# RWKV-6 and an MLP mixer on one core: the guarding branch at the end of the kernel, turned around, and a prefetch hint on TensorE

## The chip, the cores and the metric

The kernel runs on one core of one Trainium2 chip. The metric is the time of one launch on the device, in microseconds, as the median of several runs. A core has five engines with an instruction stream each: TensorE (PE; its weight loads are listed as PEld), VectorE (DVE), ScalarE (ACT), GpSimd (POOL) and SyncE (SP), which here issues nearly all transfers. [...] A profile is one further execution, recorded by the hardware. "q8" and "q14" in it are the queues on which the engines' own instructions are brought in.

## What is computed

Four sequences of 768 tokens pass through a linear attention with decay and then through a mixer over tokens and channels:

```python
for t in range(S):                      # B, H, S, D = 4, 8, 768, 48
    cur = einsum('bhd,bhe->bhde', u[None] * k[:, :, t], v[:, :, t])
    y[:, :, t] = einsum('bhd,bhde->bhe', r[:, :, t], state + cur)
    state = w[:, :, t][:, :, :, None] * state + einsum('bhd,bhe->bhde', k[:, :, t], v[:, :, t])
x = y.transpose(0, 2, 1, 3).reshape(B, S, H * D)                # 4 x 768 x 384
h = maximum(x.transpose(0, 2, 1) @ w_tok1, 0) @ w_tok2          # 768 -> 256 -> 768, over tokens
u = x + h.transpose(0, 2, 1)
out = u + maximum(u @ w_ch1, 0) @ w_ch2                         # 384 -> 1536 -> 384, over channels
```

## The kernel before

The attention is worked off in twelve units (four sequences, three units of 256 tokens each), and the mixer of a sequence follows its units. The fast way through the attention takes products of decays over a chunk of 64 tokens and divides by them. That is sound only while these products stay within a range. So each unit leaves two sums in `flags` (`ranges`, L343), which are zero when all its products lay in the range, and the kernel ends with a guard: when any flag is set, everything is computed again in another way that holds for any decay (`by_halves`, L773, in a loop over the four sequences, L838 to L840). I call this the general path. With the inputs at hand no flag is set and the general path is never entered.

The order of issue of the straight part is written out by hand: `strict` (L88) runs a list of small functions and ties every instruction to the one ahead of it on its engine. The lists are made of pieces, pairs of a weight and a function; `woven` mixes several lists in proportion to the weights. The last sequence's mixer has a list of its own, `last_mixing` (L726). Its tail is:

- `quarters(0)`, the second product of the channel mixer for rows 0 to 255, and after it `verdict` (L714): one matmul adds up the flags, VectorE reduces the 24 sums to one (L719) and turns it into a whole number, 0 or 1 (L720);
- the first product of the channel mixer for the last third of the rows;
- `quarters(1)` and `quarters(2)`, rows 256 to 511 and 512 to 767.

`quarters(s)` computes two 128-row blocks with seven products in place of eight. A product is a run of matmuls into one of two PSUM buffers (`q_ps`, L607), 24 instructions on TensorE as the trace lists them (12 weight loads, 12 matmuls), which a VectorE addition or a ScalarE copy takes out. The list it gives back has 11 pieces, in this order:

```python
return [(1.96, p1), (0.01, lambda: dve.tensor_add(s1, a21, a22)), (1.96, p4),
        (0.01, lambda: dve.tensor_sub(s2, s1, a11)), (1.96, p2), (0.01, lambda: dve.tensor_sub(a21, a11, a21)),
        (1.96, p5), (0.01, lambda: dve.tensor_sub(s4, a12, s2)), (1.96, p6), (1.96, p7), (1.96, p3)]
```

`p7` stores one row block and `p3`, the last, the other (L611, on SyncE's queue). The additions that take out the products are L617 (p1), L621 (p4), L625 (p2), L629 (p5), L633 and L634 (p6), L639 and L640 (p7) and L645 (p3).

After the straight part each engine loads the verdict into a register of its own (`values_load`, L768) and comes to the guard (L838). In the profile the guard's instructions stand on that line: compare-and-branch instructions, and waits on semaphores[...]. The program's own end follows the guard in the code; its last waits, its drains and the barrier over all engines have the line of the closing of the context, L871.

Of the kernel before, what the change touches and what calls it, by code (L numbers as in the profile page):

```python
# [12 lines left out]
i32 = mybir.dt.int32  # L13
# [3 lines left out]
ALU = mybir.AluOpType  # L17
# [28 lines left out]
def woven(*lists):  # L46

    keyed = []
    for n, pieces in enumerate(lists):
        total, at = sum(c for c, _ in pieces), 0.0  # L50
        for i, (c, f) in enumerate(pieces):
            keyed.append(((at + c / 2) / total, n, i, c, f))
            at += c
    return [(c, f) for *_, c, f in sorted(keyed, key=lambda e: e[:3])]
# [8 lines left out]
def rwkv6_then_mixer(  # L63
# [17 lines left out]
    nc = tc.nc  # L81
    pe, dve, act, pool, sp = nc.tensor, nc.vector, nc.scalar, nc.gpsimd, nc.sync
# [16 lines left out]
    const = ctx.enter_context(tc.tile_pool(name="const", bufs=1))  # L99
# [564 lines left out]
    def mixing_of(bt):  # L664
        return mixing(bt, lambda: xs[bt], lambda n: out[bt, ts(n, 128), :])
# [46 lines left out]
    flagged = []  # L712

    def verdict():  # L714
        total = bank("total")[0:1, :2 * NU]
        pe.matmul(total, ones, flags.rearrange("p i n -> p (i n)"), start=True, stop=True)
        of_all = const.tile([128, 1], f32, name="of_all")
        beyond = const.tile([128, 1], i32, name="beyond")
        dve.tensor_reduce(out=of_all[0:1], in_=total, axis=mybir.AxisListType.X, op=ALU.add)  # L719
        dve.tensor_scalar(beyond[0:1], of_all[0:1], 0.0, 1.0, op0=ALU.is_le, op1=ALU.is_lt)  # L720
        flagged.append(beyond)

    def bank(name):
        return ps_c.tile([128, 512], f32, name=name, tag="c")

    def last_mixing():  # L726
        hiddens, turned, rights, thirds, quarters = mixing_of(B - 1)
        of, sums = rights(0)
        *turned, end = turned
        pieces = [e for h in hiddens for e in h] + turned[:8] + sums[:4] + turned[8:10] + sums[4:8] + turned[10:] + sums[8:]  # L730
        ups = thirds(0, of)
        of, sums = rights(1)
        pieces += ups[:2] + [end] + ups[2:4] + woven(ups[4:], sums) + thirds(1, of)

        def third():
            L["of"], L["sums"] = rights(2)

        L = {}
        sums = [(0.05, lambda n=n: L["sums"][n][1]()) for n in range(12)]
        lefts_of = [(0.9, lambda n=n: L["ups"][n][1]()) for n in range(15)]  # L740
        pieces += [(0.01, third)] + woven(quarters(0), sums) + [(0.1, verdict), (0.01, lambda: L.update(ups=thirds(2, L["of"])))]
        return pieces + lefts_of + quarters(1) + quarters(2)

    for bt in range(B):
        ahead = []
        if bt == 0:
            to_ch = [single(e, n) for n, e in enumerate(to_ch)]
            both = [f for e in zip(ups[0], ups[1]) for f in e]
            ahead = woven(turned, sum(to_ch[:2], []))
            of_weights = [(0.1, lambda n=n: weight_sums(n)) for n in range(4)]  # L750
            pieces = woven(both, sum(to_ch[2:8], [])) + woven(downs[0][:6], to_ch[8]) + woven(downs[0][6:], of_weights[:3])
            pieces += downs[1][:4] + of_weights[3:] + downs[1][4:] + ups[2] + downs[2]
        elif bt < B - 1:
            hiddens, turned, ups, downs = mixing_of(bt)
            pieces = [e for h in hiddens for e in h] + turned
            *pieces, last = pieces
            ups[0].insert(2, last)
            for s in range(S // SEG):
                pieces += ups[s] + downs[s]
        else:  # L760
            six_banks.close()
            ps_c = six_banks.enter_context(tc.tile_pool(name="ps_c", bufs=6, space=bass.MemoryType.PSUM))
            pieces = last_mixing()
        n = (bt + 1) * UB
        att = [e for i in range(n, n + UB) if i < NU for e in steps(i)]
        strict(*(f for _, f in ahead + (woven(att, pieces) if att else pieces)))

    rare = nc.values_load(flagged[0][0:1, 0:1], min_val=0, max_val=1, skip_runtime_bounds_check_because="a comparison's result")  # L768

    six_banks.close()  # L770
    ps_g, ps_a = for_attention()
# [63 lines left out]
        for s in range(S // SEG):  # L835
            emit(ups[s] + downs[s])

    with tc.If(rare > 0, preferred_fallthrough_block=False):  # L838
        with tc.For_i(0, B, 1) as b:
            by_halves(b)  # L840

# [33 lines left out]
```

## Time and profile before

| What | us |
|---|---|
| Median of three runs | 548.63 |
| Lowest and highest of them | 548.43, 549.2 |
| The profiled execution, its own time | 550.15 |
| Its span, first to last instruction | 548.4 |
| TensorE busy in the span | 507.8 |

The profiled execution took 1.5 us more than the median of the runs; times inside it add up to its own total, not to the median. TensorE's granted clock is 0.977 of full speed over the span, and full from 122 us on. "Busy" leaves out branches, register loads, waits on semaphores and the issue of transfers. These belong to an engine's sequencer and are listed with a small q behind the engine's name; several parts of the end of this kernel consist of nothing else.

The registers of the verdict are loaded at L768 at quite different times, since each engine comes there when its own stream is through: GpSimd at 502.2 us, ScalarE at 530.7, TensorE at 539.3, VectorE at 542.4 and SyncE at 543.1.

### The profile page before, as it was taken

The page shows a single profiled execution, that of the slowest core. Times are in us where ns is not written, and L with a number is a line of the kernel's source. Part 1 is how long each engine was busy: PE and PEld are TensorE (multiplying, and loading weights), DVE is VectorE, ACT ScalarE, POOL GpSimd, SP SyncE. Part 2 cuts the span into 40 slices and gives each one's busy share as a digit, 9 for nine tenths or more (in the row PEclk, how much of TensorE's full clock was granted, in tenths as well). Part 3 has the DMA queues.
Part 4 walks back from the last instruction along what each step waited for, and adds up shares of the span by engine and source line. Part 5 has one row for each costly group of instructions (what it writes and reads, how often), then busy time and mean ns, then how long its engine had stood idle before and what let it go on. Part 6 is the DMA issues. An engine that isn't in the chain of part 4 may idle for free.

```text
span 548.4 us, 12596 instructions
## 1 busy us (share of the span) xinstructions
PE 507.8 (93%) x5542; PEld 435.3 (79%) x5542; DVE 335.8 (61%) x504; ACT 212.7 (39%) x525; POOL 1.3 (0%) x10
## 2 busy tenths in 40 slices
PE   3569899899799999999899999999999999999995
PEld 3556578666698868888888967888888968999995
DVE  7997599878772754192380665295393525775653
ACT  3676776662233333423323324413414313431300
POOL 0000000000000000000000000000000000000000
PEclk9678999899999999999999999999999999999999
DMA  8956656622231403203123113002000000000000
GB/s 304 330 165 209 182 178 241 172 89 84 87 108 34 139 17 117 59 32 125 46 78 92 45 44 99 30 1 88 1 30 1 2 29 2 1 1 31 0 31 33
DMA packets 20941, 46.01 MB, mean 84 GB/s; under 512 B 2128, under 2 KB 13008, under 8 KB 20880
## 3 DMA queue, kind: packets, MB, share of 16 engines
q1 hardware_dynamic: 20736, 45.14, 25.4%
q8 instruction: 45, 0.74, 0.6%
q14 instruction: 16, 0.13, 0.1%
q10 hardware_dynamic: 144, 0.00, 0.0%
HBM read 40.41 MB, written 4.72 MB: 82 GB/s over the span
## 4 chain that ended last, share of the span: by engine, by line
PE 72%; DVE 17%; ACT 6%; DMA 3%; issue 2%; SPq 0%; DVEq 0%; ACTq 0%
PE q_ps L607 21%; PE z_ps L518 21%; PE z_ps L550 6%; PE h_ps L494 5%; PE h_ps L501 4%; PE h_ps L589 3%; PE y_ps L306 3%; DVE to_end L354 3%; PE y_ps L320 2%; PE gram L248 2%; DMA rk<-in_rk_dram 2%; PE kv_ps L293 2%; PE gram L276 1%; DVE z L649 1%; ACT before L416 1%
## 5 line engine op out<-in xcount | busy, mean ns | idle before, releaser
L518 PE MATMUL z_ps<-xT,wch 128*128 128x256 f32 x648 | 149.1, 385 | 1.1 <-DVE o L645 1.1
L518 PEld LDWEIGHTS z_ps<-xT,wch 128*128 128x128 f32 x648 | 120.8, 191 | 18.9 <-DVE o L645 1.9
L607 PE MATMUL q_ps<-wch,z 128*128 128x192 f32 x492 | 87.4, 329 | 0.7 <-DVE o L629 0.5
L607 PEld LDWEIGHTS q_ps<-wch,z 128*128 128x128 f32 x492 | 80.3, 190 | 2.6 <-DVE o L629 1.1
L520 ACT ACTIVATE z<-z_ps 128x256 f32<-128x256 f32 x108 | 41.3, 382 | 84.8 <-PE z_ps L518 84.2
L607 PE MATMUL q_ps<-scratch,z 128*128 128x192 f32 x324 | 57.1, 328 | 3.5 <-DVE o L625 2.9
L607 PEld LDWEIGHTS q_ps<-scratch,z 128*128 128x128 f32 x324 | 52.9, 190 | 4.8 <-DVE o L625 3.8
L416 ACT ACTIVATE before<-state,to_end 112x48 f32<-112x48 f32 x176 | 44.2, 324 | 30.6 <-DVE state L426 28.0
L426 DVE TENSOR_TENSOR state<-before,kv_ps 112x192 f32<-112x192 f32 x40 | 14.0, 350 | 45.1 <-ACT before L416 29.0
L494 PE MATMUL h_ps<-x,wtok 128*128 128x384 f32 x96 | 33.9, 506 | 2.4 <-ACT x L326 2.0
L501 PE MATMUL h_ps<-h,wtok 128*128 128x384 f32 x96 | 35.4, 493 | 0.1
L503 DVE TENSOR_TENSOR x<-x,h_ps 128x384 f32<-128x384 f32 x24 | 13.3, 553 | 33.6 <-PE h_ps L501 33.4
L617 DVE TENSOR_TENSOR o<-x,z 128x192 f32<-128x192 f32 x8 | 2.9, 358 | 49.8 <-ACT z L616 46.7
L494 PEld LDWEIGHTS h_ps<-x,wtok 128*128 128x128 f32 x96 | 18.3, 195 | 14.6 <-ACT x L326 2.8
L354 DVE TENSOR_TENSOR_SCAN to_end<-w,starts 112x1041 f32<-112x1041 f32 (+1 forms) x13 | 28.1, 2160 | 2.0 <-DMA w<-in_w_dram 1.6
L362 DVE TENSOR_TENSOR_SCAN w<-w,starts 112x1041 f32<-112x1041 f32 x12 | 27.9, 2321 | 0.1
L346 ACT ACTIVATE junk<-to_end,least 112x1041 uint8<-112x1041 f32 x12 | 13.9, 1162 | 28.3 <-DVE to_end L354 28.3
L501 PEld LDWEIGHTS h_ps<-h,wtok 128*128 128x128 f32 x96 | 16.6, 190 | 9.6 <-ACT h L496 2.5
L326 ACT COPY x<-y_ps 64x384 f32<-64x384 f32 (+1 forms) x36 | 17.1, 475 | 18.3 <-PE y_ps L320 18.0
L306 PEld LDWEIGHTS y_ps<-before,rk 48*64 48x64 f32 x704 | 14.0, 144 | 12.3 <-issue 10.2
L306 PE MATMUL y_ps<-before,rk 48*64 48x48 f32 x704 | 15.4, 230 | 8.0 <-DVE state L426 8.0
L511 ACT COPY xT<-xT_ps 128x384 f32<-128x384 f32 x24 | 11.4, 476 | 22.0 <-PE xT_ps L510 22.0
(139 smaller groups left out, 668.3 us busy)
## 6 DMA issues: line engine op xcount, KB each, us to landing
rk<-in_rk_dram SPq DMA_DIRECT2D x36, 192.0 KB, 3.7
near<-in_near_dram SPq DMA_DIRECT2D x8, 768.0 KB, 4.5
w<-in_w_dram SPq DMA_DIRECT2D x11, 520.5 KB, 3.4
spare<-in_w_ch_dram SPq DMA_DIRECT2D x10, 512.0 KB, 4.8
vt<-in_v_dram SPq DMA_DIRECT2D x12, 384.0 KB, 3.8
out_dram<-o SPq DMA_DIRECT2D x24, 192.0 KB, 1.9
scratch<-in_w_ch_dram SPq DMA_DIRECT2D x8, 512.0 KB, 4.4
rk<-in_rk_dram SPq DMA_DIRECT2D x6, 512.0 KB, 8.4
```

Of the source, the lines that this page charges most:

```text
L306: pe.matmul(y[put(q, j), q, ds((c * A + a) * D, D)], r_[q * P:q * P + D, ds((c * A + a) * 128 + j * T, T)], before[g][q * P:q * P + D, a, ...
L326: return [lambda: act.copy(x[:, 0], got[:, 0])] + [lambda n=n: act.copy(x[ts(n, P), 1], got[ts(1 - n, P), 1]) for n in range(2)]
L354: dve.tensor_tensor_scan(to, of, start, 0.0, op0=ALU.mult, op1=ALU.add)
L362: dve.tensor_tensor_scan(w_[:ROWS], w_[:ROWS], starts[:ROWS], 0.0, op0=ALU.mult, op1=ALU.add)
L416: act.mul(t[:ROWS, a], state[bt, g][:ROWS, a], by_last(c, j)[:, a:a + 1])
L494: pe.matmul(sums[i], wtok1[:, c, ts(i, 128)], x_of()[:, c, :], start=(c == 0), stop=(c == C - 1))
L501: pe.matmul(ps, wtok2[:, i, ts(c, 128)], h1[:, i, :], start=(i == 0), stop=(i == DTOK // 128 - 1))
L518: pe.matmul(ps, wch1[:, m, ts(jt, 128)], xT[:, m, ts(s, SEG)], start=(m == 0), stop=(m == DM // 128 - 1))
L520: act.activation(zs[s][:, jt, :], ps, AF.Relu)
L550: pe.matmul(ps[:, q], lefts[r][:, ts(q, 128)], of[r], start=first and q == 0, stop=end and q == JB - 1, skip_group_check=True)
L589: pe.matmul(ps, zs[0][:, jt, ts(n, 128)], wch2[:, jt, :], start=(jt == 0), stop=(jt == NJ - 1))
L607: pe.matmul(ps, a[:, j, :], b[:, j, :], start=(j == 0), stop=(j == HJ - 1))
```

## The change

The verdict's number is turned around: it was 1 when a flag was set and is now 1 when none is. The guard asks for that and has an empty branch for it; the general path becomes the `Else`. In both versions the block for "false" is asked for as the one that follows the branch in the code. Before, "false" meant the end of the kernel; now it means the general path, and the block for "true", for which the general path has to be jumped over, lies behind it.

A branch hint, "LikelyTaken", for the guard's branch, which gets the label `by_halves`, is put in TensorE's stream only. It stands in the list of `quarters(2)` five pieces ahead of the end, and so just ahead of `p5`. `quarters(2)` is now called ahead of `quarters(1)`, but the pieces run in the order they had.

```diff
-        beyond = const.tile([128, 1], i32, name="beyond")
+        within_range = const.tile([128, 1], i32, name="within_range")
         dve.tensor_reduce(out=of_all[0:1], in_=total, axis=mybir.AxisListType.X, op=ALU.add)
-        dve.tensor_scalar(beyond[0:1], of_all[0:1], 0.0, 1.0, op0=ALU.is_le, op1=ALU.is_lt)
-        flagged.append(beyond)
+        dve.tensor_scalar(within_range[0:1], of_all[0:1], 0.0, None, op0=ALU.is_le)
+        flagged.append(within_range)
...
-        return pieces + lefts_of + quarters(1) + quarters(2)
+        ending = quarters(2)
+        ending.insert(-5, (0.01, lambda: tc.mark_branch_hint_location("by_halves", "LikelyTaken", [pe.engine])))
+        return pieces + lefts_of + quarters(1) + ending
...
-    rare = nc.values_load(flagged[0][0:1, 0:1], min_val=0, max_val=1, skip_runtime_bounds_check_because="a comparison's result")
+    common = nc.values_load(flagged[0][0:1, 0:1], min_val=0, max_val=1, skip_runtime_bounds_check_because="a comparison's result")
...
-    with tc.If(rare > 0, preferred_fallthrough_block=False):
+    with tc.If(common > 0, preferred_fallthrough_block=False, label="by_halves") as within_range:
+        pass
+    with within_range.Else():
         with tc.For_i(0, B, 1) as b:
             by_halves(b)
```

## The prediction, made before the changed kernel was run

> **What bounds the kernel now.** I read the page first, then the chain of waits from 535 us on, then the guard's own line (L838) and the program's closing line (L871) on every engine, then the last stores, and last the DMA records of the final microseconds.
>
> The page says that TensorE sets the time nearly everywhere, and that two queues carry nothing but instructions, q8 in pieces of 16 KB and q14 in pieces of 8 KB:
>
> ```profile
> span 548.4 us, 12596 instructions
> ...
> PE 507.8 (93%) x5542; PEld 435.3 (79%) x5542; DVE 335.8 (61%) x504; ACT 212.7 (39%) x525; POOL 1.3 (0%) x10
> ...
> q8 instruction: 45, 0.74, 0.6%
> q14 instruction: 16, 0.13, 0.1%
> ```
>
> The chain ends with the last matmul's consumer, the VectorE addition at L645, at 542.37 + 0.35 = 542.72 us:
>
> ```profile
> 534.86 7.49 PE q_ps L607 x46
> 542.35 0.02 issue
> 542.37 0.35 DVE o L645
> ```
>
> The span ends at 548.44. So 5.7 us follow in which nothing computes, and only there can a turned branch act. The guard's line and the closing line, by engine (a count, then min/median/max in ns, then first and last start in us):
>
> ```profile
> L838 ACTq COMPARE_BRANCH  x2: 38/42/45, 531.3 to 531.7; - x2
> L838 PEldq COMPARE_BRANCH  x2: 95/1954/3813, 539.9 to 542.5; - x2
> L838 DVEq COMPARE_BRANCH  x2: 51/53/55, 543.0 to 543.2; - x2
> L838 SPq COMPARE_BRANCH  x2: 38/44/49, 543.7 to 546.6; - x2
> ```
>
> ```profile
> L871 ACTq DRAIN  x2: 8/44/81, 534.2 to 548.0; - x2
> ...
> L871 SPq EVENT_SEMAPHORE  x10: 17/28/28, 547.1 to 548.4; - x10
> ```
>
> Every engine runs two branches: one that is not taken, then its waits on semaphores, then one that is taken over the general path. TensorE's second takes 3813 ns; after SyncE's second, at 546.64, its next instruction comes at 547.12. Now the stores of the last two row blocks (this view covers 500 us on):
>
> ```profile
> L611 SPq DMA_DIRECT2D out_dram<-o x6: 332/332/333, 500.4 to 542.8; - x6
> ...
> DMA to landing us min/median/max: 1.9/1.9/3.6
> ```
>
> Five land in about 1.9 us; the longest, 3.6, is the last, issued at 542.75 and landed at 546.36. SyncE's eight waits at L838 show who minds: four stand at 543.80 to 544.04, the fifth, on this store's semaphore, ends at 546.37. What the transfer does meanwhile stands in the windows (last two columns: DMA share of 16 engines, GB/s):
>
> ```profile
> 543.50:544.30 0.80, 0.00 (x0) 0.00 (x0) 0.00 (x0) 0.00 (x0) 0.00 (x0) 1.00 0.61 230
> 544.30:544.95 0.65, 0.00 (x0) 0.00 (x0) 0.00 (x0) 0.00 (x0) 0.00 (x0) 1.00 0.07 15
> 544.95:545.85 0.90, 0.00 (x0) 0.00 (x0) 0.00 (x0) 0.00 (x0) 0.00 (x0) 1.00 0.06 12
> ```
>
> A share of 0.06 is one engine of sixteen. The trace's packet records name it: a 16 KB packet of q8 runs from 543.478 to 544.923; 15 of the store's 16 parts have finished by 544.264; eight 1536-byte packets follow one after another from 544.918 and end at 545.884. TensorE's branch, which starts at 542.524, fetches its target, and the fetch stands ahead of a sixteenth of the last store. Thus two things end together: TensorE's stall (its drain starts at 546.395) and the store.
>
> [...] TensorE needs 3.87 us from the branch to its drain, ScalarE 2.52 (531.72 to 534.24); VectorE, SyncE and GpSimd[...] need 0.57, 0.48 and 0.45. [...] the held part starts as the fetch ends. [...]
>
> **The change part by part.**
>
> *The verdict.* The same VectorE instruction with one operation instead of two; 142 ns at 502.0 us, 40 us ahead of its last reader's use. Nothing.
>
> *The hint.* One instruction in TensorE's stream ahead of product p5 of the last block. TensorE's sequencer runs ahead: p3's buffer is free at 538.82 and its 24 instructions are issued by 539.27. So p2, whose buffer is free at 531.03, is issued by about 531.5, and the hint follows while 2 us of p2 and more before it are queued: hidden, cost 0. From there to the branch at 539.86 are 8.4 us against 3.87 for a fetch. No trace of before shows a hint; bounds: below, nothing; above, one whole stall of 3.87 without cover. I take 0. Its fetch at about 532.5 meets no store: those of the block before landed by 530.95, the next begin at 542.2.
>
> *The far branch, on TensorE.* It becomes the first one, 539.86, which the sequencer reaches while 2.5 us of matmuls are queued. Hinted, it should take some 0.5 us. Even if the hint did nothing, the fetch would lie at 540.81 to 542.26 (0.95 after the branch, 1.45 long) and the branch end at 543.7: away from the last store, whose packets start at 543.59, and early enough for the closing barrier. So the stall goes off the end either way.
>
> *The last store.* With no fetch ahead of it all sixteen parts should be done by 544.26; the fifteen others report by 544.62. SyncE's wait ends at about 544.63 instead of 546.37: −1.74. What is late next? SyncE itself: its register load is done at 543.64, its branch at 543.70 is now taken (0.48 instead of 0.10), its waits start at 544.18 and it comes to the fifth at 544.49. Just in time, 0.14 us ahead of the landing.
>
> *SyncE's second branch.* Today 0.48 us stand between 546.64 and 547.12, on the path that ends. If the common target runs on into the end of the program, this goes: −0.48. If a jump remains: 0. I take −0.48, since a branch over a block is what makes a second one necessary now, and the new target lies behind that block.
>
> *The other engines.* VectorE's taken branch moves from 543.20 to 543.00[...]. Bounds 0 and +0.54; I take 0. ScalarE's stall of 2.5 us at 531 and GpSimd's branch at 503 have over 10 us of cover in either order.
>
> Sum: −1.74 − 0.48 = −2.22. The closing waits and the barrier (547.12 to 548.44) stay as they are. The profiled execution took 550.15: 548.44 of span and 1.71 around it. It would take 546.22 + 1.71 = 547.93. The median shown is 548.63, 1.52 below the profiled one; the same saving gives 546.4.
>
> **The rivals.**
>
> *A, as worked out*: 546.4, own range 545.8 to 547.1 (the three runs before span 0.8). Chance 0.70.
>
> *B, a part only*: VectorE's fetch takes the place of TensorE's in front of the last packets (+0.54), a jump remains (+0.48), or both: −1.7 to −1.2, down to −0.5 if some other piece of the closing turns up late: 547.0 to 548.1. For it: the margin of SyncE is 0.14 us, and VectorE's fetch comes 0.1 us ahead of the store's end. Against: one DMA engine in sixteen. Chance 0.14.
>
> *C, no gain to be seen*: [...] At ScalarE's price (2.52) its waits start at 546.22, the fifth passes at once, and the closing waits start at about 546.8 instead of 547.12: −0.3, so 548.3. For it: the change moves the target by some ten instructions. Against: the distance over the general path is the same, and SyncE's jump made it without a stall today. The same time results if the collision is an affair of the profiled execution alone. Chance 0.08.
>
> *D, slower*: [...] Before, no fetch lies between 522.30 and 543.48, [...] with nothing queued to cover it all of this stands on the path: −2.22 + 3.87 = +1.65, 550.3. It decides from a loss of 2.2 + 1.1 = 3.3 us up. Against: two microseconds of queued product usually cover part of it. Chance 0.08.
>
> **How the numbers follow.** A has 0.70, B 0.14, C 0.08, D 0.08. The likeliest is A, 546.4. With A, and B nearly whole, less their tails, the range 545.8 to 548.1 holds about 0.8. A measurement here tells 0.2%, 1.1 us, from no change: faster means below 547.5. A nearly whole and two thirds of B: 0.79. Within 0.2%: the rest of B, C and a bit of D: 0.13. Slower: D, 0.08.
>
> **What would show it.** Right: one branch per engine at L838 where there were two; none of TensorE's above 1 us; a 16 KB packet on q8 near 532; the last store landing in about 1.9 us; SyncE's closing waits starting near 544.9. Hint without effect but A still true: TensorE's branch at 539.9 takes 3.8 us and the end is early all the same. B: a second branch on SyncE, or a lone 8 KB packet ahead of the store's last ones. C: SyncE's branch followed by a gap of 2.5 us. D: a gap in TensorE's products between 531 and 540. Wrong altogether: the last store still lands after 546.

## The result, and the profile after

The changed kernel takes 547.14 us (median of eight runs, 545.73 to 547.86), the kernel before 548.58 in the same comparison (eight runs, 548.06 to 549.2). The ratio is 0.9968, with a 95% interval of 0.9953 to 0.9983: faster by 1.4 us, by this measurement somewhere between 0.9 and 2.6. The profiled execution took 547.47 us with a span of 545.8.

The guard's line, L840 now, on four engines of the changed kernel (a count, then min/median/max in ns, then first and last start in us), with the hint, which the trace puts on the closing's line:

```profile
L840 ACTq COMPARE_BRANCH  x1: 50/50/50, 530.8 to 530.8; - x1
L840 ACTq EVENT_SEMAPHORE  x1: 17/17/17, 533.4 to 533.4; - x1
L840 PEldq COMPARE_BRANCH  x1: 397/397/397, 539.4 to 539.4; - x1
...
L840 DVEq COMPARE_BRANCH  x1: 72/72/72, 542.6 to 542.6; - x1
...
L840 SPq COMPARE_BRANCH  x1: 45/45/45, 543.3 to 543.3; - x1
```

```profile
L875 SPq EVENT_SEMAPHORE  x10: 17/28/28, 544.5 to 545.7; - x10
...
L875 PEldq BRANCH_PREFETCH_HINT  x1: 45/45/45, 531.0 to 531.0; - x1
```

Where each engine ran two branches there is one. TensorE's takes 397 ns where its second one took 3813. SyncE's closing waits begin at 544.5, right behind its last wait at the guard:

```profile
L840 SPq EVENT_SEMAPHORE  x8: 17/17/17, 543.8 to 544.4; - x8
```

The stores from 500 us on:

```profile
L611 SPq DMA_DIRECT2D out_dram<-o x6: 332/332/333, 499.9 to 542.3; - x6
...
DMA to landing us min/median/max: 1.8/1.9/2.0
```

The longest is no longer 3.6 us. The windows of the last store (last three columns: granted clock, DMA share of 16 engines, GB/s) show all its parts together:

```profile
543.10:543.85 0.75, 0.00 (x0) 0.00 (x0) 0.00 (x0) 0.00 (x0) 0.00 (x0) 1.00 0.71 262
543.85:544.75 0.90, 0.00 (x0) 0.00 (x0) 0.00 (x0) 0.00 (x0) 0.00 (x0) 0.59 0.05 18
```

What is left in the second window are two pieces of 8 KB on q14 (543.95 to 544.26 and 544.34 to 544.75); the store's last packet ends at 543.84. The chain of waits still closes with the same addition:

```profile
541.93 0.02 issue
541.95 0.35 DVE o L645
```

From its start to the end of the span I count "the end" of the kernel, and I cut it in three: until the last store is issued, until its last part has landed, and from there on (times of the semaphore records in the trace).

| us | L645 to issue | issue to landing | landing to end | the end |
|---|---|---|---|---|
| before | 0.38 | 3.61 | 2.08 | 6.07 |
| after | 0.38 | 1.86 | 1.58 | 3.82 |

So the end is 2.25 us shorter, 1.75 of it in the store and 0.50 behind it. The spans differ by 2.7; the other 0.4 is the straight part, which came to L645 at 541.95 instead of 542.37.

### The profile page after: what moved, and what is told of

The parts are those of the page before. It is cut to its first block, busy times and chain, and to the rows that moved or that the text cites. A ratio compares the mean times of both kernels' runs of the same rounds, so it can differ in the third digit from the quotient of the medians.

```text
span 545.8 us, 12592 instructions
## 1 busy us (share of the span) xinstructions
PE 508.5 (93%) x5542; PEld 436.2 (80%) x5542; DVE 336.0 (62%) x504; ACT 212.7 (39%) x525; POOL 1.3 (0%) x10
## 4 chain that ended last, share of the span: by engine, by line
PE 71%; DVE 18%; ACT 5%; issue 2%; DMA 2%; SPq 0%; DVEq 0%; ACTq 0%
PE q_ps L607 21%; PE z_ps L518 21%; PE z_ps L550 6%; PE h_ps L494 5%; PE h_ps L501 4%; DVE to_end L354 3%; PE h_ps L589 3%; PE y_ps L306 2%; PE y_ps L320 2%; PE gram L248 2%; PE kv_ps L293 2%; PE gram L276 1%; DVE w L362 1%; DMA rk<-in_rk_dram 1%; DVE z L649 1%
```

## The experiments

Each run was timed in five rounds against the kernel before; ratios are against that, with their 95% intervals. The table has the parts of the end in each one's profile. The runs are told below it.

| Kernel | L645 at | to issue | to landing | to end | the end | Ratio |
|---|---|---|---|---|---|---|
| before, again | 541.84 | 0.38 | 3.04 | 2.09 | 5.51 | 1.0005 (0.9994 to 1.0017) |
| after, again | 541.30 | 0.38 | 1.85 | 1.58 | 3.82 | 0.9949 (0.9932 to 0.9967) |
| after, third time | 542.00 | 0.38 | 1.86 | 1.58 | 3.82 | 0.9968 (0.9957 to 0.9979) |
| no hint | 539.67 | 0.38 | 1.86 | 1.58 | 3.82 | 0.9967 (0.9952 to 0.9981) |
| turned, order in the code kept | 541.39 | 0.38 | 3.64 | 2.08 | 6.11 | 1.0003 (0.9990 to 1.0016) |
| late verdict, no hint | 541.59 | 0.38 | 2.80 | 1.58 | 4.76 | 0.9972 (0.9956 to 0.9988) |
| late verdict, hint | 540.85 | 0.38 | 2.70 | 1.58 | 4.66 | 0.9981 (0.9971 to 0.9991) |
| path cut to a matmul | 541.64 | 0.38 | 1.86 | 1.05 | 3.30 | 0.9955 (0.9936 to 0.9974) |
| no guard | 541.21 | 0.38 | 1.86 | 1.02 | 3.26 | 0.9932 (0.9912 to 0.9953) |
| cut path with loads, two branches | 542.30 | 1.49 | 1.85 | 1.05 | 4.40 | 0.9972 (0.9955 to 0.9989) |
| cut path with loads, turned | 540.49 | 1.31 | 1.86 | 1.05 | 4.22 | 0.9964 (0.9951 to 0.9977) |
| path's transfers on ScalarE | 540.65 | 0.38 | 1.87 | 1.58 | 3.84 | 0.9969 (0.9956 to 0.9981) |

**Do the ends repeat?** Before and after, unchanged.

> The kernel before, unchanged, once more, to see how far the length of its end repeats. I call 'end' the time from the start of the last addition (L645) to the end of the span: 6.07 us in the profile of before, 3.81 in that of after. My theory (TensorE's target page is fetched ahead of a sixteenth of the last store) expects 5.8 to 6.2 again, with the last store landing in 3.3 to 3.7 us. The rival that the collision was a chance of that one execution expects an end near 4.4 and a last store of 1.9 us.

> The changed kernel, unchanged, once more. Theory: the end (from the start of L645 to the end of the span) is again 3.8 us, and its median stands 2.2 us under that of before; if the first comparison's 1.44 us is the true size, then the end of before is on average shorter than the 6.07 us of its profile, or the rest of the kernel became slower by 0.8 us.

> The changed kernel once more, on the chip of these three, for comparison: end 3.82 us, last store 1.86 us, time 2.2 us under before within the scatter of the straight part (in the profiles so far the start of L645 lies anywhere from 539.7 to 542.4 us).

After repeats to 0.01 us. Before does not: the collision is there again, but the fetch (543.00 to 544.18 in this execution) took 1.18 us instead of 1.45, and the store landed in 3.04 instead of 3.61, below what I had expected. This is the longest of the stores from 520 us on in that run, and the windows of its two stretches; in the second, which at a share of 0.05 is again for the most part the work of a single DMA engine of sixteen, the store's last packets run until 544.80:

```profile
DMA to landing us min/median/max: 1.8/1.9/3.0
```

```profile
543.05:543.80 0.75, 0.00 (x0) 0.00 (x0) 0.00 (x0) 0.00 (x0) 0.00 (x0) 1.00 0.66 246
544.20:545.00 0.80, 0.00 (x0) 0.00 (x0) 0.00 (x0) 0.00 (x0) 0.00 (x0) 1.00 0.05 13
```

Over the three profiles with the old order in the code (before, before again, and the order-kept run below) the end is 6.07, 5.51 and 6.11, 5.90 on average, 2.08 above after's 3.82. The three comparisons of medians (the first and the two repetitions of after) give 1.44, 2.24 and 1.61 us.

**Hint or layout?** Two edits of the changed kernel, the second on top of the first:

```diff
-        ending.insert(-5, (0.01, lambda: tc.mark_branch_hint_location("by_halves", "LikelyTaken", [pe.engine])))
```

```diff
-    with tc.If(common > 0, preferred_fallthrough_block=False, label="by_halves") as within_range:
+    with tc.If(common > 0, preferred_fallthrough_block=True, label="by_halves") as within_range:
```

> The changed kernel without the hint. Theory: TensorE's branch, at about 539.4, now takes 3.8 us, its fetch lies at about 540.5 to 541.9, ahead of the last store's packets, the last store lands in 1.9 us, and the end is 3.8 us as with the hint: no difference in time to after (within 0.3 us). Rival (the hint brings the gain): the end is 5.6 us, 1.7 slower than after.

> The changed kernel without the hint and with the block for 'true' as the one that follows the branch: the comparison is turned, the layout in the code is that of before. Theory (only the place of the common target counts): two branches per engine, TensorE's second at 542.5 takes 3.8 us, end 6.0 us, time that of before. Rival (the comparison or the empty block counts): the end of after, 3.8 us.

Both came out as the theory had it. Without the hint, TensorE's branch and the wait behind it:

```profile
L839 PEldq COMPARE_BRANCH  x1: 3885/3885/3885, 537.2 to 537.2; - x1
...
L839 PEldq EVENT_SEMAPHORE  x1: 51/51/51, 541.1 to 541.1; - x1
```

The whole stall of 3.9 us is back, but it begins at 537.2, 2.5 us ahead of L645. The 16 KB fetch on q8 runs from 538.70 to 539.62, ahead of the last store but one instead of the last. That store lands in 2.3 us, at 540.98, and SyncE waits for it only at 541.76. The end is 3.82 as with the hint. With the order kept, the two branches and the long store are back:

```profile
L839 PEldq COMPARE_BRANCH  x2: 92/2021/3950, 538.9 to 541.5; - x2
L839 SPq COMPARE_BRANCH  x2: 38/44/49, 542.7 to 545.7; - x2
```

These two runs have the same operations and differ in the order of the two blocks in the code alone, with which go the place of the common target and the number of branches. That order carries the whole effect; the direction of the comparison, the empty block and the hint carry none of it that shows. They also part the 0.50 from the rest: behind the landing the end is 1.58 in one, 2.08 in the other. SyncE's last wait at the guard (545.63) and its first closing wait (546.18) lie 0.55 us apart where the second branch stands between them, and 0.07 where it doesn't (542.13 and 542.19). SyncE's closing waits with the order kept, and without the hint:

```profile
L874 SPq EVENT_SEMAPHORE  x10: 17/28/28, 546.2 to 547.4; - x10
```

```profile
L874 SPq EVENT_SEMAPHORE  x10: 17/28/28, 542.2 to 543.4; - x10
```

**Is it the time of the fetch?** The verdict moved to just ahead of p3, so that TensorE comes late to its branch in spite of the new layout; once without the hint, once with it:

```diff
-        pieces += [(0.01, third)] + woven(quarters(0), sums) + [(0.1, verdict), (0.01, lambda: L.update(ups=thirds(2, L["of"])))]
+        pieces += [(0.01, third)] + woven(quarters(0), sums) + [(0.01, lambda: L.update(ups=thirds(2, L["of"])))]
...
         ending = quarters(2)
+        ending.insert(-1, (0.1, verdict))
```

> The changed kernel without the hint and with the verdict moved from the end of quarters(0) to just ahead of p3, the last product: each engine comes to its register load later, TensorE to its branch at about 542.3 instead of 539.4. Theory (the time of the fetch counts): the fetch lies at about 543.2 to 544.6, ahead of the last store on one DMA engine; the last store lands in 3.3 to 3.6 us and the end is 5.5 us, 1.7 above after. Rival (with the branch turned, the end is short in any case): 3.8 us. ScalarE's branch now lies at about 542.3 too, and its stall of 2.5 us ends at about 545, near the closing; it can add 0 to 0.3 us.

> As the run with the late verdict and no hint, but with the hint where the change has it. Theory: TensorE's page is fetched near 532, its branch takes 0.4 us, the last store lands in 1.9 us and the end is 3.8 to 4.4 us, the upper end where ScalarE's stall or ScalarE's own fetches show: 1.2 to 1.7 us faster than without the hint. Rival (the hint does nothing): no difference to the run without it.

Without the hint the collision is back, though with one branch per engine: the last store lands in 2.80 us. It is less than I had expected, since TensorE came to its branch at 541.1 and not at 542.3. The q8 fetch ran from 542.24 to 543.48, the store's packets started at 542.80, and so the fetch held its sixteenth for 0.7 us and not for 1.3. The windows of this run, the store together and the held part (two 8 KB fetches of q14, from 543.57 and from 543.98, are in the second share):

```profile
542.70:543.45 0.75, 0.00 (x0) 0.00 (x0) 0.00 (x0) 0.00 (x0) 0.00 (x0) 1.00 0.68 246
543.45:544.30 0.85, 0.00 (x0) 0.00 (x0) 0.00 (x0) 0.00 (x0) 0.00 (x0) 1.00 0.12 34
```

With the hint I was wrong. TensorE's branch is short, as expected, and yet the store lands late:

```profile
L841 PEldq COMPARE_BRANCH  x1: 397/397/397, 540.4 to 540.4; - x1
```

```profile
DMA to landing us min/median/max: 1.8/1.9/2.7
```

A 16 KB fetch on q8 had begun at 530.68. But 1.13 us after the start of the branch there is one more: 541.53 to 542.70, again ahead of the store, whose packets started at 542.06. The packet records don't say what either fetch carries; I take both for TensorE's, by their place behind its hint and its branch. With the hint the branch took 0.40 us, against 3.67 in the run without it, and this second transfer came all the same. With an early verdict it lies at 540.55 to 541.72 in after, 1.11 us behind the start of the branch and ahead of every packet of the last two stores. In the third profile of after it ran from 541.04 to 542.00, into the last store but one, which landed in 2.27 us; nobody waits for that one yet, and the end was 3.82 all the same.

**What is SyncE's second branch worth by itself, and the rest of the guard?** In the kernel before, the body of the general path was replaced:

```diff
-        with tc.For_i(0, B, 1) as b:
-            by_halves(b)
+        pe.matmul(ps_a.tile([128, 2, 512], f32, name="y_ps", tag="a")[:1, 0, :1], ones, ones, start=True, stop=True)
```

> The kernel before, in which the general path is left out but for one matmul (it isn't entered with these inputs)[...]; the two branches per engine stay. Theory: TensorE's second branch takes about 0.5 us, nothing is fetched ahead of the last store, which lands in 1.9 us, while SyncE's second branch stays on the path: end 6.07 - 1.74 = 4.3 us. Rival (the second branch is the gain): end 5.6 to 6.1 us. Second rival (SyncE's 0.48 costs nothing, the store is all): 3.8 us.

TensorE's two branches in this run, and the landing of its stores from 520 us on:

```profile
L838 PEldq COMPARE_BRANCH  x2: 90/135/180, 539.1 to 541.8; - x2
```

```profile
DMA to landing us min/median/max: 1.8/1.9/2.0
```

TensorE's second branch takes 180 ns, and the last store lands in 1.86 us, with two branches per engine: the first half of the theory holds. For the second half the run doesn't serve. The store is issued at 542.02, behind SyncE's two branches at 541.64 and 541.74, as I take it because a path that writes no output no longer holds it ahead of the guard. SyncE has no waits at the guard in this run, and the end is 3.30, lower than any of the three values expected. I tried to mend this with eight loads on SyncE's queue in the path, once with the guard of before and once turned:

```diff
+        for b in range(2):
+            x = xpool.tile([128, C, DM], f32, name="x")
+            for c in range(4):
+                sp.dma_start(x[:, c], v[b, ts(c, 128), :])
```

> The kernel before, in which the general path is cut to one matmul and eight loads on SyncE's queue (the rest is left out; it isn't entered with these inputs), so that SyncE keeps its waits for the last store at the guard and its second branch after them[...]. Theory (store 1.74, SyncE's second branch 0.48): last store 1.9 us, from its landing to the end of the span 2.08 us as in before, end from L645 on 4.3 us. Rival[...]: 1.6 us after the landing, end 3.8 to 3.9 us.

> The same cut path, with the guard turned as in the change and no hint. Theory: one branch per engine, from the landing to the end of the span 1.58 us as in after, end 3.82 us: 0.5 us less than with two branches, from SyncE's second branch alone. Rival: no difference between the two.

The waits were back, but the store still lay behind the guard (issued 1.49 and 1.31 us after L645). Their ends, 4.40 and 4.22, miss the 4.3 and 3.82 that were expected. The difference of 0.18 between the two is all in that first part, and neither run tests the 0.50 behind the landing. What shows it stays the pair of no hint and order kept.

> The kernel before without guard, register loads and general path, which are left out. It bounds what a guard can still cost: SyncE comes straight from the last store to the closing waits, of which the store's is the fifth. Theory: the store's 1.86 us from issue to landing sets the end, which is 3.81 less three waits of the guard (0.20) and four of the closing (0.25), 3.3 to 3.4 us: 0.4 to 0.5 us faster than after. Rival (the register loads and branches still cost): 1 us or more faster than after.

This came near what was expected, 3.26 where it was 3.3 to 3.4: of after's end 0.56 us is the guard's. In after SyncE passes the guard's wait for the last store at 544.20 and the closing's wait for the same store at 544.72, with seven other waits between the two; without the guard the closing's wait follows 0.02 us behind the landing. So nearly all of the 0.56 are waits that stand behind the landing. The ratio of this run, 0.9932, is lower than after's by more than that; the intervals allow 0.5 us.

> The changed kernel, hint included, with all transfers of the general path issued by ScalarE instead of SyncE (the straight part is as it was). Theory: after's remaining excess over a kernel without a guard (3.82 against 3.26 us) is SyncE's eight waits at the guard, of which five come at or after the last store's landing; with no transfer of SyncE's in the general path they go, SyncE waits for the store only at the closing, and the end is 3.3 us, 0.5 us faster than after and some 2.8 faster than before. Rival (the waits only move to ScalarE, or the closing grows): 3.8 us or more.

```diff
+        out_queue = act if bt is None else sp
...
-                sp.dma_start(out_rows(2 * s + n), L["o"][:, n])
+                out_queue.dma_start(out_rows(2 * s + n), L["o"][:, n])
...
-            sp.dma_start(r_, rk[ds(b * UB + half, 1), 0].rearrange("o p n -> p (o n)"))
+            act.dma_start(r_, rk[ds(b * UB + half, 1), 0].rearrange("o p n -> p (o n)"))
```

The other loads and stores of the general path are changed in the same way.

My theory of the guard's waits fell. SyncE keeps all eight of them, though the general path issues nothing on its queue any more, and the end stays at 3.84:

```profile
L841 SPq EVENT_SEMAPHORE  x8: 17/17/17, 542.2 to 543.1; - x8
```

What sets these waits, I can't say from these runs. None of them gave a kernel with the guard whole that beats after.

## Why the prediction was right, step by step

**The bottleneck and the collision: right.** The span's last microseconds were bound by a sixteenth of the last store behind TensorE's fetch: the store landed in 3.61 us with it and in 1.86 without. The store's term was given as −1.74 and is −1.75 between the two profiles; so near a match is luck, as the last point shows. Shown: the collision comes back with the old layout, it comes back in part with the new layout and a late verdict, and it is gone with the old layout and a path cut to a matmul (where the store lies behind the guard, though).

**SyncE's second branch: right**, −0.48 given and −0.50 measured: SyncE's first closing wait, at 544.5, follows its last wait at the guard with no branch between them.

**The hint: right that it costs nothing, and that the gain doesn't need it.** It was executed at 531.04 (about 531.5 expected) and a 16 KB fetch on q8 followed, from 532.24 to 533.50. The branch took 0.40 us, and without the hint the end was 3.82 us as with it. TensorE is busy through the stretch where rival D expected a gap of 3.87 us, as this window of after shows (second value: 10.00 us of TensorE in 10):

```profile
530.00:540.00 10.00, 10.00 (x64) 10.00 (x63) 5.81 (x10) 0.32 (x1) 0.00 (x0) 1.00 0.02 6
```

**VectorE's fetch: no cost, by a margin that the prediction didn't have.** In before an 8 KB fetch of q14 ran from 544.36 to 544.90, which by its distance from the branch I take for VectorE's. It was expected about 0.2 us earlier, through the store's last 0.1 us, with bounds of 0 and 0.54, and was put at 0, with the one argument that both would have to be on the same DMA engine of sixteen. In after it ran from 543.95, 0.12 us behind the store's last packet. In before it had started 1.16 us after VectorE's taken branch, here 1.37; in the two repetitions of after it came 0.07 and 0.04 us behind the last packet. The trace doesn't show what the longer distance comes from, and whether an overlap would have cost anything was not tested. **SyncE arrives just in time: right**, its fourth wait, at 544.05, is 0.14 us ahead of the landing, and rival C's stall of SyncE, 2.5 us, did not occur: from its branch at 543.30 to the wait at 543.78 are the 0.48 us of before.

**The size in the medians: inside what the comparisons can tell, with the store's term taken from one execution.** The expected 2.22 us lie inside the intervals of all three comparisons (0.9 to 2.6, 1.8 to 3.7 and 1.2 to 2.4 us), so the 1.44 of the first shows no term to be wrong by itself. The profiles show one that varies, the store's 1.74. I took it from one execution, whose fetch of 1.45 us was among the longest on q8 in that trace (45 fetches of 0.88 to 1.46 us, median 1.04). In the second profile of before the fetch took 1.18, and the term is 1.19 (3.04 − 1.85). With the mean over the three profiles of the old layout the end gains 2.08 us and not 2.22. The end of after is alike to 0.01 us in all its profiles. How the rest of the difference divides between the end of before in other executions and the straight part stays open: L645 starts anywhere from 539.67 to 542.37 in these profiles, though the instructions ahead of it are nearly the same, and what moves it stays open too.

## What to carry to other kernels

At the end of a kernel, ask of every taken branch which transfers its instruction fetch meets, not only how long its own engine stalls: the costly part here, 1.75 us of 2.25, was the store next to it, on another engine's queue. Put the guard's far branch where work is still queued, and its common target so that it runs on into the end. The hint added nothing here, where the stall had cover (an end of 3.82 us with it and without), and it didn't stop the further fetch 1.1 us behind the branch. And take the size of a collision from more than one execution: in two of the kernel before the fetch took 1.45 and 1.18 us, and the store landed in 3.61 and 3.04.

## What the runs showed of the hardware

The 24 stores in the trace of before show by themselves that a 16 KB instruction fetch held one sixteenth of a store where the two met. Where fifteen parts landed within 1.9 us of the issue, the sixteenth landed within 1.9 too, except in six stores, at 2.5 to 3.6 us, and just these six met a q8 fetch. At the end of the kernel the last part landed 1.1 to 1.4 us after the fetch had ended, in all five profiles with such a meeting.

A branch that wasn't taken took about 0.1 us from its start to the next instruction's (SyncE in before: 543.70 to 543.80). A taken one took 0.18 on SyncE when it jumped over the cut path with loads (540.48 to 540.67, turned), 0.48 over the whole one, and again 0.18 over the whole one once its transfers were ScalarE's (542.00 to 542.18): in these three runs the price on the engine went with what the path holds for it.

With the hint, a 16 KB fetch on q8 ran 7 us ahead of TensorE's branch (532.24 to 533.50 in after, the branch at 539.44), in a stretch where the trace of before has none (from 522.30 to 543.48), and the branch took 0.40 us in place of 3.89 in the run without the hint.
